# Closing TensorE's loop in the middle of an output slot, and alternating short and full pieces in the second score fill

## The chip, the core and the metric

The kernel runs on one core of a Trainium2 chip. The metric is the time of one execution on the device in microseconds (us). Repeats of one kernel scatter by 0.1 to 1%.

## The reference

```python
B, H, Sq, Sk, D = 16, 32, 192, 1024, 128          # bf16
def reference(q, k, v):
    scores = jnp.einsum("bhqd,bhkd->bhqk", q, k) * D ** -0.5
    return jnp.einsum("bhqk,bhkd->bhqd", softmax(scores), v)
```

There are 512 heads. The kernel treats four at a time, a *quad*, so there are 128 quads.

## The kernel before

For each quad, TensorE makes three *score fills*. A fill computes 512 columns of scores (keys on the partitions, queries along the columns) for each of the four heads into four PSUM banks. A column block of 192 queries of one key tile does not divide 512, so the fills are cut into pieces; `CUTS` lists them as (key tile, first query, end query). Between the fills stand *value slots*: half a quad's outputs need 1.5 slots, so there are three slots a quad too. ScalarE takes the exponential of each fill (one instruction for the bank of the first head, one for the other three), VectorE normalizes each slot's output.

The lines that matter, shortened (`step(f)` is written out as its two calls, "..." marks what is left out):

```python
CUTS = (
    ((0, 0, 192), (1, 0, 192), (2, 0, 128)),
    ((2, 128, 192), (3, 0, 192), (4, 0, 192), (5, 0, 64)),     # the second fill
    ((5, 64, 192), (6, 0, 192), (7, 0, 192)),
)
...
def take(s, c):
    pe.wait_ge(s, c).then_inc(s, -c)
def qk(f):                                    # a score fill
    x, b = divmod(f, 3)
    if b == 0:
        take(s_qt, 1)
    take(s_kt, 1)
    take(s_e1, 1)                             # the first head's bank has been read
    for t, n0, n1 in CUTS[b]:
        for w in range(4):                    # one pass: four matmuls, 32 rows each, one per head
            for a in range(4):
                ins = pe.matmul(S[:, c0: c0 + n1 - n0], kt[...], qt[...], start=w == 0, ...)
    ins.then_inc(s_qk, 1)
def pv(s):                                    # a value slot: 32 matmuls in pairs of 64 columns
    x, i = divmod(s, 3)
    if i == 0:
        take(s_e3, 3)                         # the exps of this quad
        take(s_vp, 2)                         # its values
    ...
        take(s_on, 1)                         # the last slot has been normalized
    ...
    ins.then_inc(s_pv, 1)
with nc.Fori(0, NF // (3 * R), engines=[PE], head_slot={PE: 100}):
    for f in range(3 * R):                    # two quads in one turn of the loop
        qk(f)
        pv(f - LAG)                           # LAG = 4: the slot that follows fill 1 begins a quad
```

Each `take` is one instruction of TensorE's *sequencer*, the part of the engine that works through waits, takes and branches and hands the matmuls to TensorE's queue. And the slot that follows the second fill is the one with `i == 0`: three takes (the exps, the spread values, the normalized slot) stand between that fill and that slot, where the other fills have one.

## Time and profile before

| | before |
|---|---|
| median, range | 841.78 us, 841.64 to 842.84 (3 runs) |
| span of the profiled run | 840.2 us |
| TensorE busy, ScalarE busy | 98%, 89% |
| quad to quad, quads 4 to 90 | 6.329 us |

First the page of the profile: a busy line (us, share of the span, instructions), the DMA rate in 40 slices of the span, and groups of instructions (busy time, mean ns of one, then the engine's idle time before them and what ended most of it). L613 is the fills' matmul, L632 the slots', L777 and L780 are the exps.

```profile
PE 821.0 (98%) x32910; PEld 735.3 (88%) x32910; DVE 599.6 (71%) x1288; ACT 748.4 (89%) x770; POOL 549.9 (65%) x646
GB/s 329 399 401 404 404 404 406 403 405 401 389 400 401 392 401 386 397 396 399 386 392 392 391 400 400 382 400 401 382 400 396 392 398 392 394 389 397 393 159 43
L780 ACT ACTIVATE f_pt<-f_s 128x1536 bf16<-128x1536 f32 x384 | 554.9, 1445 | 0.0
L632 PE MATMUL f_o<-f_vp,f_pt 128*64 128x129 bf16 x12320 | 433.5, 222 | 3.0 <-issue 2.9
L613 PE MATMUL f_s<-f_qt,f_kt 32*128 32x192 bf16 (+2 forms) x20480 | 423.6, 226 | 6.6 <-PEq L597 3.8
L777 ACT ACTIVATE f_pt<-f_s 128x512 bf16<-128x512 f32 x384 | 229.2, 597 | 79.3 <-PE f_s L613 71.3
```

TensorE has next to no idle time and ScalarE waits for it, so TensorE sets the pace. But "busy" here counts from the first matmul's start to a modelled end, so short holes between matmuls hide in it. The timeline of TensorE around one turn of the loop shows them (columns: start us, duration us, engine, line, what, how many):

```profile
407.85 1.09 PE L613 MATMUL f_s<-f_qt,f_kt 32*128 32x128 bf16 x48
408.87 1.13 PE L632 MATMUL f_o<-f_vp,f_pt 128*64 128x129 bf16 x32
409.99 1.10 PE L613 MATMUL f_s<-f_qt,f_kt 32*128 32x192 bf16 x48
411.02 1.11 PE L632 MATMUL f_o<-f_vp,f_pt 128*64 128x129 bf16 x32
412.06 1.11 PE L613 MATMUL f_s<-f_qt,f_kt 32*128 32x64 bf16 x64
413.17 0.34 PE L632 MATMUL f_o<-f_vp,f_pt 128*64 128x129 bf16 x5
```

The durations overlap; the starts are what counts. From slot to next fill is 411.02 to 412.06 = 1.04 us in a plain place, but 408.87 to 409.99 = 1.12 us where the loop closes. And the second fill (x64) takes 412.06 to 413.17 = 1.11 us, where the first takes 1.03 and the third 1.02, for the same 2048 query columns per head.

In the rest of this text a *gap* is the time from the start of the last matmul of a fill or slot to the start of the first one of the next, by the start times in the trace, averaged over quads 30 to 125. Within a fill, passes start 85 ns apart for 192 queries, 57 for 128 and 29 for 64.

### The profile page before, as it was taken

Reading aid. Unit: us, or ns where it says so; the run is one execution under the profiler, and the core shown is the slowest. Engines: PE = TensorE matmul, PEld = TensorE weight load, DVE = VectorE, ACT = ScalarE, POOL = GpSimd, SP = SyncE. Lnnn points to the kernel's source line nnn. Section 1 sums busy time; section 2 is a strip of 40 time slices with the busy share of each in tenths; the row PEclk is TensorE's granted clock in tenths of the full one; section 3 lists DMA queues with packets and bytes.
Section 4 is the critical chain, followed back from the end, with each engine's and each line's share of the span. In section 5 each row is a group of like instructions: output and inputs, shape, how many; then the busy total and the mean of one; then the engine's idle time right before and its main releaser. Section 6 shows DMA issues by size and latency. Waiting matters only on the chain. (4 is left out here: it accounts for less than half of the span.)

```text
span 840.2 us, 71522 instructions
## 1 busy us (share of the span) xinstructions
PE 821.0 (98%) x32910; PEld 735.3 (88%) x32910; DVE 599.6 (71%) x1288; ACT 748.4 (89%) x770; POOL 549.9 (65%) x646
## 2 busy tenths in 40 slices
PE   6999999999999999999999999999999999999995
PEld 4789898988888989988988888988998998888885
DVE  5577777777777777777777777777777777777763
ACT  5699999999999999999999999999999999999994
POOL 6566666666666766766766666666666666676671
PEclk9899999999999999999999999999999999999999
DMA  8999999999999999999999999999999999999941
GB/s 329 399 401 404 404 404 406 403 405 401 389 400 401 392 401 386 397 396 399 386 392 392 391 400 400 382 400 401 382 400 396 392 398 392 394 389 397 393 159 43
DMA packets 139213, 319.21 MB, mean 380 GB/s; under 512 B 7200, under 2 KB 57376, under 8 KB 122912
## 3 DMA queue, kind: packets, MB, share of 16 engines
q1 hardware_dynamic: 139168, 318.80, 99.3%
q14 instruction: 39, 0.32, 0.1%
q8 instruction: 6, 0.10, 0.1%
HBM read 293.60 MB, written 25.17 MB: 379 GB/s over the span
## 5 line engine op out<-in xcount | busy, mean ns | idle before, releaser
L780 ACT ACTIVATE f_pt<-f_s 128x1536 bf16<-128x1536 f32 x384 | 554.9, 1445 | 0.0
L571 POOL COPY f_kt<-f_kx 128x768 uint32<-128x768 uint32 (+1 forms) x384 | 293.7, 784 | 269.9 <-DVE f_kx L696 140.7
L632 PE MATMUL f_o<-f_vp,f_pt 128*64 128x129 bf16 x12320 | 433.5, 222 | 3.0 <-issue 2.9
L613 PE MATMUL f_s<-f_qt,f_kt 32*128 32x192 bf16 (+2 forms) x20480 | 423.6, 226 | 6.6 <-PEq L597 3.8
L632 PEld LDWEIGHTS f_o<-f_vp,f_pt 128*64 128x64 bf16 x12320 | 373.3, 110 | 46.2 <-issue 24.0
L613 PEld LDWEIGHTS f_s<-f_qt,f_kt 32*128 32x128 bf16 x20480 | 357.7, 92 | 46.5 <-issue 10.1
L696 DVE STREAM_TRANSPOSE f_kx<-f_kn 128x768 uint32<-128x768 uint32 (+1 forms) x384 | 334.0, 870 | 10.5 <-DMA f_kn<-in_k_dram 10.5
L777 ACT ACTIVATE f_pt<-f_s 128x512 bf16<-128x512 f32 x384 | 229.2, 597 | 79.3 <-PE f_s L613 71.3
L580 POOL COPY f_vp<-f_vs 128x1024 uint32<-128x1024 uint32 x256 | 259.5, 1043 | 5.1 <-PE f_o L632 5.0
L717 DVE RECIPROCAL f_rinv<-f_o 128x2 f32<-128x2 f32 x381 | 65.1, 171 | 206.6 <-PE f_o L632 206.6
L721 DVE TENSOR_TENSOR f_ob<-f_o,f_rinv 128x256 bf16<-128x256 f32 x381 | 161.7, 424 | 13.3 <-DVE f_rinv L717 0.3
L705 DVE STREAM_TRANSPOSE f_qt<-f_qn 128x384 uint32<-128x384 uint32 x128 | 72.8, 569 | 0.0
L661 PE MATMUL f_o<-f_ones 128*128 128x512 bf16 x12 | 4.1, 512 | 1.1 <-POOL f_ones L562 1.1
L661 PEld LDWEIGHTS f_o<-f_ones 128*128 128x128 bf16 x12 | 1.4, 127 | 3.2 <-issue 1.7
L677 DVE MEMSET f_pt<- 128x3072 uint32 x1 | 2.6, 2618 | 1.5 <-PEq L806 1.5
L563 POOL MEMSET f_vp<- 128x4160 uint32 x1 | 3.6, 3569 | 0.0
L632 PE MATMUL f_s<-f_vp,f_pt 128*64 128x129 bf16 x96 | 3.2, 220 | 0.3 <-PEq L597 0.3
L632 PEld LDWEIGHTS f_s<-f_vp,f_pt 128*64 128x64 bf16 x96 | 2.9, 110 | 0.4 <-issue 0.4
L769 ACT ACTIVATE f_pt<-f_ones 128x3072 f32<-128x3072 bf16 x1 | 2.8, 2763 | 0.0
L769 ACT ACT_TABLE_LOAD x1 | 1.3, 1283 | 0.8 <-PEq L806 0.8
L717 DVE RECIPROCAL f_rinv<-f_s 128x2 f32<-128x2 f32 x3 | 0.5, 171 | 1.4 <-PE f_s L632 1.4
L671 PE MATMUL f_o<-f_bad,f_ones 128*1 128x1 bf16 x1 | 0.2, 164 | 1.3 <-DVEq L761 1.3
(13 smaller groups left out, 5.3 us busy)
## 6 DMA issues: line engine op xcount, KB each, us to landing
f_vs<-in_v_dram SPq DMA_DIRECT2D x128, 1024.0 KB, 9.0
f_kn<-in_k_dram SPq DMA_DIRECT2D x127, 1024.0 KB, 11.1
f_qn<-in_q_dram SPq DMA_DIRECT2D x128, 192.0 KB, 10.3
out_dram<-f_ob SPq DMA_DIRECT2D x63, 384.0 KB, 11.4
f_kn<-in_k_dram SPq DMA_DIRECT2D x1, 640.0 KB, 6.7
f_kn<-in_k_dram SPq DMA_DIRECT2D x1, 384.0 KB, 3.9
out_dram<-f_ob SPq DMA_DIRECT2D x2, 192.0 KB, 2.3
```

The source lines that it names most:

```text
L571: gp.tensor_copy(kt[:, x % NKT].bitcast(U32).rearrange("p U (j s u) c -> p U j s (u c)", s=2, u=2)[:, lo:hi], kx[:, x % 2].rearrange("p (U ...
L580: gp.tensor_copy(vp[:, x % NVP, 2 * T * i: 2 * T * i + 2 * T, 0:D].bitcast(U32), vs[:, x % NVS, 2 * i: 2 * i + 2, :].rearrange("p a (t d) ...
L613: ins = pe.matmul(S[:, c0: c0 + n1 - n0], kt[r, x % NKT, 2 * t + h, :, c], qt[r, x % R, h, n0:n1, c], start=w == 0, stop=w == 3, tile_posi ...
L632: return pe.matmul(O[m0: m0 + m, u, 0:129], pt[:, x % R, 2 * y + z, t * SQ + n0: t * SQ + n0 + m], vp[:, x % NVP, (2 * y + z) * T + t, 0:129],
L661: pe.matmul(o_ps[:].rearrange("p a b -> p (a b)"), ones[:], ones[:].unsqueeze(1).to_broadcast([128, 4, 128]), start=True, stop=True)
L696: dve.transpose(kx[:, x % 2].rearrange("p (U s j u) -> p s u U j", s=2, j=32, u=2)[:, :, :, lo:hi], kn[:, x % NKN].rearrange("p (s u U i) ...
L705: dve.transpose(qt[:, x % R].bitcast(U32).rearrange("p b (y j u) c -> p u y b (j c)", y=3, u=2), qn[:, x % NKN].rearrange("p (u y b i) -> ...
L717: dve.reciprocal(ri, O[:, :, 128]).then_inc(s_rc, 1)
L721: dve.tensor_tensor(ob[:, so, 6 * a + 2 * w: 6 * a + 2 * w + 2, :], O[:, :, 0:128], ri.unsqueeze(2).to_broadcast([128, 2, D]), ALU.mult,). ...
L769: act.activation(pt[:, 1].rearrange("p a c -> p (a c)").bitcast(F32), ones[:, 0:1].to_broadcast([128, 2 * T * SQ]), ACT_FN.Copy).then_inc( ...
L777: act.activation(pt[:, x % R, 0, c], s1_ps[:], ACT_FN.Exp, scale=scale).then_inc(s_e1, 1)
L780: act.activation(pt[:, x % R, 1:4, c], s3_ps[f % 2][:], ACT_FN.Exp, scale=scale).then_inc(s_e3, 1)
```

## The change

The intent is to hide two costs of TensorE's sequencer. (The diff is shortened; the first and third line of `CUTS` get the same nesting and keep their order.) The loop's register step and branch now stand between the two halves of a value slot, so that queued matmuls cover them. And the second fill no longer ends with four short passes in a row: its passes alternate, full (192 queries), short (64), full, short, so that the last passes last longer. No matmul is added or removed in the steady part; an extra half slot runs once at the start, and one is made up for behind the loop. The thresholds on `s_pv` rise by one (`BLANK`) for the blank slot.

```diff
-    ((2, 128, 192), (3, 0, 192), (4, 0, 192), (5, 0, 64)),
+    (((3, 0, 192), (2, 128, 192)), ((4, 0, 192), (5, 0, 64))),
...
+    BLANK = LAG + 1
...
-                    for t, n0, n1 in CUTS[b]:
-                        c0 = t * SQ + n0 - 512 * b
+                    for group in CUTS[b]:
                         for w in range(4):
...
+                            for g, (t, n0, n1) in enumerate(group):
+                                c0 = t * SQ + n0 - 512 * b
+                                for a in range(4):
...
-                                    start=w == 0, stop=w == 3, tile_position=(32 * a, 0))
+                                        start=w == 0 and g == 0, stop=w == 3, skip_group_check=True,
+                                        tile_position=(32 * a, 0))
...
-                def pv(s):
+                def pv(s, blocks=(0, 1)):
...
-                    ins.then_inc(s_pv, 1)
+                    if 1 in blocks:
+                        ins.then_inc(s_pv, 1)
...
+                    pv(-1 - LAG, (1,))
                     for f in range(3 * R):
-                        step(f)
-                for f in range(NF, NF + LAG):
-                    step(f)
+                        qk(f)
+                        pv(f - LAG, (0,) if f == 3 * R - 1 else (0, 1))
+                pv(NF - 1 - LAG, (1,))
+                for s in range(NF - LAG, NF):
+                    pv(s)
```

## The prediction

> **What bounds the kernel.** TensorE. The page's busy line gives PE 98%, ACT 89%, DVE 71%, POOL 65%. In the steady part (windows 40 to 790 us) PE is busy 99.9% at granted clock 1.00. Successive quads of heads (three fills each) start 6.33 us apart in the trace. ScalarE is a close second: its two exps take 597 + 1445 ns a fill, 6.13 us a quad, and before the first it waits 0.15 to 0.21 us for TensorE's scores (timeline at 400 to 420). DMA moves 393 to 404 GB/s and looks full, but K lands about 10 us before its transpose in mid-run, and that lead grew while DMA ran at 404: about 6.15 us a quad is its floor. So TensorE can gain about 0.18 us a quad before another wall.
>
> **Where TensorE loses time.** Start times of single matmuls show steady passes: 85 ns for 192 queries, 57 for 128, 29 for 64, 59 for a pair of value matmuls. Each switch between score tiles (32 rows) and value tiles (64 columns) costs about 90 ns beyond the last pass. The Trainium skill, "TensorEngine Tiling (Array Packing)", section "Key Properties", says that changing the tiling mode drains TensorE; these gaps agree. Two gaps are longer than the drain, because the sequencer is late:
> 1. *Loop edge.* Value slot to score fill takes 225 ns (mean) from last matmul start to first where the loop closes, 153 elsewhere. The sequencer gets there only 340 ns into the value slot, because the queue holds it back; then come a 102 ns register step, a 207 ns branch and three semaphore takes of about 150 ns. Loss 72 ns x 64 = 4.6 us.
> 2. *After the second fill.* Three takes follow it. The sequencer leaves the fill 260 ns before its last matmul starts, because the queue then holds the last six passes (two of 85, four of 29). The gap is 161 ns, where 29 + 90 = 118 would do. Loss 43 ns x 128 = 5.5 us.
>
> **What the change does.** It adds and removes no matmuls in the loop (half a dummy slot before the first fill, about 0.5 us, hidden under the first load). At the edge only half a slot (32 instructions) is queued before the branch, so the sequencer should reach it without queueing, run the branch under the queued matmuls, and catch up: the first gap goes to about 153 ns, 4.6 us saved. Alternating makes the last six passes three of 85 and three of 29, 56 ns longer, so the takes are ready before the drain ends: second gap 118 to 130 ns, 4 to 5.5 us. The fill itself (919 to 924 ns, first to last matmul) stays or loses about 10 ns. Everything else waits on TensorE and follows; ACT's idle time shrinks, DMA needs about 399 GB/s.
>
> **Sum.** All of it is on the critical path; about 122 of 128 quads are in the steady part. 8 to 11 us at best; I take 9: **832.8 us**, range 828.5 to 837.5. Chances: faster by over 2% 0.02, within 2% 0.96, slower 0.02.
>
> **What shows each step.** Quad period 6.25 us instead of 6.33; loop-edge gap 153; gap after second fill under 130; ACT's idle before its first exp down from 79 us to about 70; DMA 398 to 400 GB/s in mid-run; busy times of ACT, DVE and POOL unchanged.
>
> **What would make it wrong.** Half a slot is too little cover and TensorE starves in mid-slot after the branch (a hole of tens of ns between the halves); alternating 192- and 64-query passes breaks the 29 ns pace, because a weight load no longer hides under a short pass; instruction fetch stalls elsewhere in the rotated loop; or an exp becomes late and its wait replaces the gap.

## The result, and the profile after

The changed kernel takes 837.22 us (median of 4 runs, 836.53 to 839.74), against 841.71 us before in the same rounds. The ratio is 0.995, with a 95% interval of 0.9927 to 0.9973. A ratio is the mean time of one kernel's fast runs over that of the other's of the same rounds, so it is not quite the ratio of the medians. The gain is 4.5 us, where 9 were forecast.

The page of the changed kernel, the lines that answer to those above (L616 fills, L638 slots, L782 and L785 exps):

```profile
PE 818.2 (98%) x32926; PEld 726.0 (87%) x32926; DVE 599.3 (72%) x1288; ACT 748.6 (90%) x770; POOL 550.0 (66%) x646
L785 ACT ACTIVATE f_pt<-f_s 128x1536 bf16<-128x1536 f32 x384 | 554.6, 1444 | 1.8 <-PE f_o L638 1.8
L638 PE MATMUL f_o<-f_vp,f_pt 128*64 128x129 bf16 x12336 | 434.3, 222 | 1.8 <-issue 1.8
L616 PE MATMUL f_s<-f_qt,f_kt 32*128 32x192 bf16 (+2 forms) x20480 | 421.6, 226 | 5.9 <-issue 3.4
L782 ACT ACTIVATE f_pt<-f_s 128x512 bf16<-128x512 f32 x384 | 229.3, 597 | 72.6 <-PE f_s L616 37.8
```

Its TensorE timeline around one turn of the loop:

```profile
405.56 1.09 PE L616 MATMUL f_s<-f_qt,f_kt 32*128 32x128 bf16 x48
406.58 1.13 PE L638 MATMUL f_o<-f_vp,f_pt 128*64 128x129 bf16 x32
407.64 1.10 PE L616 MATMUL f_s<-f_qt,f_kt 32*128 32x192 bf16 x48
408.67 1.11 PE L638 MATMUL f_o<-f_vp,f_pt 128*64 128x129 bf16 x32
409.72 1.09 PE L616 MATMUL f_s<-f_qt,f_kt 32*128 32x192 bf16 x64
410.79 0.42 PE L638 MATMUL f_o<-f_vp,f_pt 128*64 128x129 bf16 x8
```

The slot in which the loop closes now lasts 406.58 to 407.64 = 1.06 us instead of 1.12: that half of the change did what it should. The second fill lasts 409.72 to 410.79 = 1.07 us. By the forecast of fill and gap it was to come down to 1.03 to 1.05.

The two stretches from the start of quad 4 to that of quad 124 contain nearly the whole difference. In the windows view (start:end, length, then busy us and instructions of each engine, granted clock, DMA share, GB/s) the kernel before and then the changed one:

```profile
43.02:802.29 759.27, 758.66 (x30723) 682.00 (x30721) 556.87 (x1200) 697.88 (x721) 511.69 (x601) 1.00 1.03 396
```

```profile
42.74:797.62 754.88, 754.86 (x30723) 672.70 (x30721) 556.65 (x1200) 697.87 (x721) 511.76 (x602) 1.00 1.04 399
```

The same work (30723 matmuls, ScalarE 697.9 us) fits in 4.4 us less. The clock was full in both.

### The profile page after: what moved, and what is told of

The parts are those of the page before. It is cut to its first block, busy times and chain, and to the rows that moved or that the text cites. A ratio compares the mean times of both kernels' runs of the same rounds, so it can differ in the third digit from the quotient of the medians.

```text
span 835.6 us, 71554 instructions
## 1 busy us (share of the span) xinstructions
PE 818.2 (98%) x32926; PEld 726.0 (87%) x32926; DVE 599.3 (72%) x1288; ACT 748.6 (90%) x770; POOL 550.0 (66%) x646
## 2 busy tenths in 40 slices
DMA packets 139213, 319.21 MB, mean 382 GB/s; under 512 B 7200, under 2 KB 57376, under 8 KB 122912
## 5 line engine op out<-in xcount | busy, mean ns | idle before, releaser
L785 ACT ACTIVATE f_pt<-f_s 128x1536 bf16<-128x1536 f32 x384 | 554.6, 1444 | 1.8 <-PE f_o L638 1.8
L638 PE MATMUL f_o<-f_vp,f_pt 128*64 128x129 bf16 x12336 | 434.3, 222 | 1.8 <-issue 1.8
L616 PE MATMUL f_s<-f_qt,f_kt 32*128 32x192 bf16 (+2 forms) x20480 | 421.6, 226 | 5.9 <-issue 3.4
L638 PEld LDWEIGHTS f_o<-f_vp,f_pt 128*64 128x64 bf16 x12336 | 373.9, 110 | 53.7 <-issue 23.5
L616 PEld LDWEIGHTS f_s<-f_qt,f_kt 32*128 32x128 bf16 x20480 | 347.6, 92 | 43.0 <-issue 6.5
L782 ACT ACTIVATE f_pt<-f_s 128x512 bf16<-128x512 f32 x384 | 229.3, 597 | 72.6 <-PE f_s L616 37.8
L638 PE MATMUL f_s<-f_vp,f_pt 128*64 128x129 bf16 x96 | 3.1, 220 | 0.3 <-PEq L599 0.3
L638 PEld LDWEIGHTS f_s<-f_vp,f_pt 128*64 128x64 bf16 x96 | 2.9, 110 | 0.4 <-issue 0.4
```

The lines of the kernel that those rows point to most:

```text
L616: ins = pe.matmul(S[:, c0: c0 + n1 - n0], kt[r, x % NKT, 2 * t + h, :, c], qt[r, x % R, h, n0:n1, c], start=w == 0 and g == 0, stop=w == 3 ...
L638: return pe.matmul(O[m0: m0 + m, u, 0:129], pt[:, x % R, 2 * y + z, t * SQ + n0: t * SQ + n0 + m], vp[:, x % NVP, (2 * y + z) * T + t, 0:129],
L782: act.activation(pt[:, x % R, 0, c], s1_ps[:], ACT_FN.Exp, scale=scale).then_inc(s_e1, 1)
L785: act.activation(pt[:, x % R, 1:4, c], s3_ps[f % 2][:], ACT_FN.Exp, scale=scale).then_inc(s_e3, 1)
```

## The experiments

All times below are medians. This table has what the traces and the times gave; the gaps are means over quads 30 to 125, ns. Each ratio is to the kernel before in the same rounds.

| kernel | gap at the loop edge | second fill, first to last start | gap after it | quad, 4 to 90, us | time, us | ratio to before |
|---|---|---|---|---|---|---|
| before | 225 | 921 | 161 | 6.329 | 841.71 | 1 |
| the changed kernel | 153 | 904 | 169 | 6.291 | 837.22 | 0.995 |
| its repeat, after_again | 153 | 904 | 169 | 6.291 | 837.40 | 0.9948 |
| edge_only | 153 | 923 | 167 | 6.304 | 838.60 | 0.9965 |
| alt_only | 209 | 905 | 169 | 6.318 | 841.94 | 1.0003 |
| head_132 | 211 | 921 | 155 | 6.319 | 841.34 | 0.9999 |
| short_last | 153 | 918 | 386 | 6.518 | 866.67 | 1.0299 |
| short_first | 153 | 865 | 171 | 6.248 | 834.78 | 0.9917 |
| extra_wait | 153 | 904 | 169 | 6.291 | 838.05 | 0.9954 |
| extra_take | 153 | 905 | 321 | 6.434 | 855.79 | 1.0166 |
| takes_first | 153 | 905 | 115 | 6.234 | 834.10 | 0.9903 |
| takes_first_again | 153 | 905 | 115 | 6.234 | 834.36 | 0.9913 |
| takes_edge | 153 | 924 | 117 | 6.252 | 834.35 | 0.9919 |
| takes_half_v (wrong result) | 153 | 905 | 115 | 6.234 | 831.94 | 0.9884 |

One more source of scatter must be known to read the last two columns together: the start, while the first loads arrive. In the traces the fifth quad (quad 4) began between 42.7 us (the changed kernel) and 45.3 us (extra_take) after the span's start; two traces of the very same changed kernel had 42.7 and 44.3. A kernel may gain 1.3 us in its quads and show nothing in its time.

### Each half alone: edge_only and alt_only

edge_only is the changed kernel with the second fill in its old order:

```diff
-    (((3, 0, 192), (2, 128, 192)), ((4, 0, 192), (5, 0, 64))),
+    (((2, 128, 192),), ((3, 0, 192),), ((4, 0, 192),), ((5, 0, 64),)),
```

> Only the loop's closing point is moved; the second fill keeps the old order of its pieces (64, 192, 192, 64). If the two halves of the change add up, the gap at the loop edge is 153 ns as in the changed kernel, the gap after the second fill stays at the 161 ns of the kernel before (151 to 183), the quad period is about 6.29 us, and the time 838 us, 0.995 to 0.996 of before. If the alternation brought a real share of the 4.5 us, this kernel is 1 to 4 us slower than the changed one.

alt_only is the kernel before with the changed `CUTS` and the changed loop in `qk`, and nothing else.

> Only the second fill alternates; the loop closes at the end of a value slot as before. Expected: loop-edge gap 211 to 254 ns as before, second fill 904 ns from first to last matmul start and a gap of 169 ns after it as in the changed kernel, period about 6.32 us, time 840 to 841.5 us. Over 2 us gained would mean that the alternation is worth something by itself.

They ran in the same rounds as a repeat of the changed kernel:

> The changed kernel once more, on the same chip and in the same rounds as the three others, as their yardstick: 837 us, 0.995 of before.

The repeat took 837.40 us, 0.9948 (0.9934 to 0.9963). edge_only took 838.60 us, 0.9965 (0.9953 to 0.9977), with the loop-edge gap at 153 ns. The trace's records of the sequencer show the cover (means over the 48 loop edges of quads 30 to 125). In the kernel before, the register step begins 340 ns into the slot, the branch ends 650 ns in, and the last take begins 1023 ns in, 117 ns after the slot's last matmul. In the changed kernel these are 22, 332 and 789 ns, and the last take begins 119 ns before the slot's last matmul. alt_only took 841.94 us, 1.0003 (0.999 to 1.0016). In the quads the parts add up nearly: 6.329 to 6.304 (25 ns) for the edge, 6.329 to 6.318 (11 ns) for the alternation, 38 ns for both. So the loop edge brought most of the gain, and the alternation about 11 ns a quad, 1.3 us in the quads of its trace. Its time does not show even that; its profiled run reached quad 4 at 44.4 us, against 43.0 before, and lost as much there.

Those 11 ns are not the ones that were forecast, and the shorter fill did not bring them either. The fill became 17 ns shorter and the gap after it 8 ns *longer*: as the experiments below show, in both kernels the slot starts when the takes are done, wherever the fill ends before that. From the fill's first matmul to the slot's first one it takes 1082 ns before and 1073 ns in the changed kernel. The first take comes at the same time in both (662 and 660 ns). What differs is the two spacings between the three takes: together 314 ns before, where some takes are spaced 186 ns instead of 156, and 307 ns in the changed kernel, where none are. In alt_only the gaps at the loop edge became regular too (209 ns instead of 225 in the mean). The next experiment gets nearly the same without alternating.

### Is it the place in the fetch blocks? head_132

Moving the loop's closing point also moves every instruction of the loop against its head. `head_slot` sets the place at which the loop's first instruction stands in the block of instructions in which it is loaded. The kernel before, with the head 32 places later:

```diff
-                             head_slot={mybir.EngineType.PE: 100}):
+                             head_slot={mybir.EngineType.PE: 132}):
```

> The kernel before with its loop's first instruction loaded 32 places later in the fetch block, so that nearly all of the loop stands in the blocks as it does in the changed kernel. If the gain at the loop edge is the cover of queued matmuls, nothing changes: edge gaps 211 to 254 ns, 841 to 842 us. If it came from where the instructions fall in the blocks, the edge gap falls toward 153 ns and the time toward 837 us. The irregular quads (6.42 us instead of 6.35) may change in number: worth under 1.5 us.

The edge gap is 211 ns, far from 153, and the time 841.34 us, 0.9999 (0.9983 to 1.0016). So the gain at the edge comes from the cover; this one other place does not bring it. The place has a small effect of its own. At slot 100, 15 of 48 edge gaps of the kernel before are about 254 ns and the rest about 210; at 132 only one is that long. And at 132 no take after the second fill is spaced 186 ns instead of 156, so that fill and gap last 1076 ns together instead of 1082. In the quads that is worth 10 ns, which is what alt_only gained (6.319 and 6.318 us). Either change makes the sequencer's steps regular; beyond that, alternation is not shown to bring more than the 3 ns between 1076 and 1073. Why the steps are irregular is open: edge_only, whose instructions stand in the same places as those of the changed kernel, has such takes too (its two spacings are 321 ns together).

### What the gap after the second fill waits for: takes_first and extra_take

The gap is 169 ns. Theory 1: the sequencer comes late, because three takes stand there. Rival: this is the *drain*, the time that TensorE needs between the last pass of score tiles and the first of value tiles, and it is that long when a full pass stands just before the last short one. takes_first moves two of the takes ahead of the fill, where the sequencer has to wait for the exp anyhow:

```diff
                     take(s_kt, 1)
+                    if b == 1:
+                        take(s_e3, 3)
+                        take(s_vp, 2)
                     take(s_e1, 1)
...
-                    if i == 0:
+                    if i == 0 and s >= NF - LAG:
                         take(s_e3, 3)
                         take(s_vp, 2)
```

> The changed kernel, with the takes of the third exps and of the spread values moved from behind the second fill to ahead of it, so that one take is left between the fill and its value slot. Theory 1 (the gap of 169 ns is the sequencer, late by two takes): the gap falls to about 118 ns, the period to 6.24 us, the time to about 831 us, 0.987 of before. Rival (169 ns is what TensorE needs to drain when a 192-query pass stands just before the last short pass): the gap stays at 169 ns and the time at 837 us.

The gap fell to 115 ns in every quad, and the quads to 6.234 us. The timeline of TensorE in it, the second fill and what follows:

```profile
408.05 1.09 PE L619 MATMUL f_s<-f_qt,f_kt 32*128 32x192 bf16 x64
409.07 1.13 PE L641 MATMUL f_o<-f_vp,f_pt 128*64 128x129 bf16 x32
```

From the fill to the slot it is now 1.02 us. Theory 1 holds and the rival falls. (The one take that is left comes 777 ns into the fill, later than the first of the three did. It is the take of the normalized slot, whose normalization ends 739 ns in. The value slot starts only 243 ns after it, so it costs nothing.) The time is 834.10 us, 0.9903 (0.9883 to 0.9923), 3 us more than expected; that is the subject of takes_half_v.

The opposite dose is one more wait in that place. The first attempt changed nothing:

```diff
                         take(s_vp, 2)
+                        pe.wait_ge(s_one, 1)
```

> The changed kernel with one more wait, long satisfied, between the second fill and its value slot. If the sequencer is what the gap waits for, each thing added to it shows in full: the gap grows from 169 ns by the wait's own cost, 50 to 150 ns, and the time by 128 times that, 6 to 19 us. If the gap is TensorE's drain, with the sequencer only just in time by chance, it grows as well but by less than the wait's spacing in the trace.

The gap stayed at 169 ns, the time at 838.05 us. The trace shows why: no instruction was added. The wait was joined to the take that follows (`take(s_on)`), which then waits for two semaphores at no visible cost. So the test did not test; mended, with a count so that it has to stand alone:

```diff
+                        pe.wait_ge(s_one, 1).then_inc(s_dum, 1)
```

> The dose test again, mended: the single added wait of the run before made no instruction of its own. Here one more long satisfied take, which also counts up a semaphore that nobody reads, stands between the second fill and its value slot of the changed kernel. If the gap waits for the sequencer, it grows by one take's spacing, from 169 to about 320 ns, and the time by about 128 x 0.151 = 19 us, to about 857 us. If the gap is the drain, with the takes hidden inside it, it grows by less than 100 ns and the time by less than 13 us.

```profile
407.71 1.09 PE L617 MATMUL f_s<-f_qt,f_kt 32*128 32x192 bf16 x64
408.94 0.77 PE L640 MATMUL f_o<-f_vp,f_pt 128*64 128x129 bf16 x20
```

From the fill to the slot it is now 1.23 us: the gap grew from 169 to 321 ns, one take's spacing in full. The quad grew by 143 ns (6.291 to 6.434 us; some 10 ns came back in other fills and slots), and the time to 855.79 us. So nearly all of each take in this place is paid for, in each of the 128 quads.

### When the sequencer can leave a fill: short_last and short_first

That leaves the question why alternating did not bring the takes forward. In the trace's records of the sequencer, the first take after the second fill comes 662 ns after the fill's first matmul before, and 660 ns after it in the changed kernel. The forecast wanted it some 56 ns earlier, relative to the last matmul. One theory: the queue lets the sequencer go at a certain pass. Rival: the sequencer needs a fixed time for the fill's 128 instructions. The two tests put all short passes last, and all first:

```diff
-    (((3, 0, 192), (2, 128, 192)), ((4, 0, 192), (5, 0, 64))),
+    (((3, 0, 192),), ((4, 0, 192),), ((2, 128, 192),), ((5, 0, 64),)),     # short_last
+    (((2, 128, 192),), ((5, 0, 64),), ((3, 0, 192),), ((4, 0, 192),)),     # short_first
```

> The changed kernel with the order of the second fill's pieces 192, 192, 64, 64: all eight short passes last. Theory (the sequencer can leave the fill only some 105 ns after its tenth pass has started, because until then the queue is full): the tenth pass is then a short one, starting about 720 ns into the fill, the first take comes at about 825 ns, the value slot starts about 414 ns after that, so the gap after the fill is about 335 ns, 21 us more in all: about 858 us. Rival (the sequencer needs a fixed time for the fill's 128 instructions, 957 ns after the take that lets it in, whatever TensorE does): first take at 660 ns as now, gap 168 ns, 837 us.

> The changed kernel with the order 64, 64, 192, 192: all eight short passes first. Theory of the full queue: the tenth pass starts about 330 ns into the fill, the first take comes at about 435 ns, the takes are over long before the fill is, and the gap is the drain alone after a 192-query pass, 171 ns as after the third fill, with the last matmul starting 850 ns after the first instead of 904; the period falls by about 50 ns to 6.24 us, the time to 831 us. Rival of the fixed time: first take at 660 ns and value slot at 1073 ns as now, 837 us. If the short passes at the start find the queue empty, they run slower than 29 ns each, and part of the gain is lost: then 832 to 836 us.

In short_last it is 1.30 us from the second fill to the slot, and the profile itself now calls the rest a wait for the sequencer ("PEq"):

```profile
411.77 1.11 PE L616 MATMUL f_s<-f_qt,f_kt 32*128 32x192 bf16 x64
413.07 0.74 PE L638 MATMUL f_o<-f_vp,f_pt 128*64 128x129 bf16 x19 [0.19 <-PEq L599]
```

The time is 866.67 us, 1.0299 (1.0284 to 1.0314). The first take comes 886 ns into the fill. In short_first it comes 465 ns in, long before the fill's end, and the gap of 171 ns is the drain alone; the time is 834.78 us, 0.9917 (0.9892 to 0.9943). The rival of the fixed time (660 ns in all orders) falls. (831 us were expected, or 832 to 836 if the short passes began slowly. They did: the first ones start 40 and 32 ns apart instead of 29, and the fill lasts 865 ns instead of 850. Its quads run at 6.248 us up to quad 90 and at 6.304 us from 90 to 124, where it waits for K as takes_first does below.)

My number was off, though: 335 ns of gap were expected in short_last, and 386 came. The four orders together say at which pass the sequencer is let go. Of the passes' starts, that of the ninth of the 16 lies at the most even distance from the take. It starts at (ns after the first matmul), and the first take comes at (differences taken before rounding):

| order of the second fill | 9th pass starts | first take | difference |
|---|---|---|---|
| before | 474 | 662 | 187 |
| alternating | 468 | 660 | 191 |
| short passes last | 695 | 886 | 192 |
| short passes first | 251 | 465 | 214 |

Measured from the tenth pass the differences would scatter from 103 to 164 ns, from the eighth from 221 to 276. So it is the ninth pass, not the tenth: when the take comes, the matmuls of the last eight passes have not ended, or not for more than 10 ns, by the trace's modelled ends. That is 32 matmuls and their 32 weight loads. The Trainium skill, "TensorE: Matmul & The Clock Gate", gives TensorE a queue of 64 entries in the table at its head; these runs agree with 64 if an entry is held until its matmul has ended, which the page doesn't say and no run shows directly.

With that the gap can be worked out. After the first take come two more spacings (156 + 151 ns), then 107 ns to the first value matmul, by the records of before and after. The slot can start 187 + 307 + 107 = 601 ns after the ninth pass at the earliest. Before: 474 + 601 - 921 = 154 ns (161 measured, the mean with some takes spaced 186 ns). Changed: 468 + 605 - 904 = 169 ns (169). Short passes last: 695 + 606 - 918 = 383 ns (386). The 605 and 606 are 601 with those orders' own differences, 191 and 192 ns, in place of 187.

In both the old order and the alternating one, the last eight passes are four full and four short. Alternating shuffles them within the queue's reach and so cannot give the sequencer more time.

### Where takes_first lost its last 3 us: takes_half_v and takes_edge

takes_first ran its quads at 6.234 us up to quad 90 and at 6.351 us from 90 to 124. The lines of the windows view for 100 to 300 and 600 to 780 us, and the wait of VectorE's transposes for K (total us, times, longest):

```profile
100.00:300.00 200.00, 199.98 (x8210) 178.72 (x8204) 148.69 (x320) 186.61 (x194) 136.97 (x162) 1.00 1.04 404
600.00:780.00 180.00, 177.48 (x7273) 158.42 (x7264) 132.61 (x285) 164.88 (x171) 120.75 (x143) 1.00 1.03 393
```

```profile
DVE f_kx L704 <- DMA f_kn<-in_k_dram: 25.3, 32, 3.4
```

TensorE's busy time falls below its window in the second stretch, and DMA moves 393 GB/s. Worked out from the 319.21 MB of the page, quads of 6.234 us need 400. K landed 6 to 8 us before its use from quad 6 to quad 54, the lead then shrank by about 0.2 us a quad, and from quad 96 on it was 0.02 us: the transposes waited for each load. The test takes a fifth of the traffic away, with a wrong result on purpose (relative error 0.91):

```diff
+                    g = 4 if x < NVS else 2
                     e.dma_start(
-                        vs[:, x % NVS, :, :],
-                        vf[4 * x:4 * x + 4].rearrange("a (m t) d -> m a (t d)", t=T),
+                        vs[:, x % NVS, 0:g, :],
+                        vf[4 * x:4 * x + g].rearrange("a (m t) d -> m a (t d)", t=T),
```

> Wrong result on purpose: the version with two takes moved ahead of the second fill, loading only half of V from the sixth quad on, so that DMA has a fifth less to move. That version ran at 6.23 us a quad until K's lead was used up near quad 90, then at 6.35. If DMA is the wall that it met, the quads stay at 6.23 to 6.24 us to the end, K's lead stays above 5 us, and the time is 829 to 831 us with little scatter. If something else stretched those quads (the stores' buffers, ScalarE, the vector engine), they are as long as before and the time is about 834 us.

```profile
600.00:780.00 180.00, 180.00 (x7408) 160.94 (x7402) 134.51 (x290) 167.94 (x174) 122.92 (x145) 1.00 0.93 317
```

```profile
DVE f_kx L705 <- DMA f_kn<-in_k_dram: 10.3, 5, 3.3
```

The quads stay at 6.23 us to the end, K's lead at 12 to 15 us, and the later waits for K are gone; the 10.3 us that are left, in five waits, are the start's, as in the kernel before, which has this line:

```profile
DVE f_kx L696 <- DMA f_kn<-in_k_dram: 10.5, 5, 3.5
```

DMA is the wall. The time, 831.94 us, 0.9884 (0.9866 to 0.9901), is 1 us above the expected range; its profiled run came late out of the start (quad 4 at 44.9 us).

The last pair asks whether the alternation is worth anything when the sequencer is in time. takes_edge has the takes moved, the loop closed in mid-slot, and the old order of the fill:

> The two takes moved ahead of the second fill and the loop closed in mid-slot, but the second fill in its old order 64, 192, 192, 64: is the alternation worth anything once the sequencer is no longer late? Expected: gap after the second fill about 118 ns, from first to last matmul of the fill 921 ns against 904, so quads of about 6.25 us until DMA's lead is used up, and a time within 2 us of the alternating one (832 to 836 us).

It ran beside a repeat of takes_first:

> The alternating version with the two takes ahead of the fill once more, as the yardstick of these rounds, on the chip that they run on: 831 to 836.5 us; quads of 6.23 us as long as K's lead lasts.

takes_edge took 834.35 us, 0.9919 (0.9901 to 0.9936), the repeat 834.36 us, 0.9913 (0.9886 to 0.994). The quads still differ by 18 ns as long as the lead lasts (6.252 and 6.234 us), but with DMA at its limit the times are the same. takes_first beats the changed kernel of the same rounds, 0.9903 against 0.9948 with intervals that do not meet.

## Why the prediction was right and wrong

The time fell inside the range (837.22 us; 828.5 to 837.5), but only by 0.3 us and at its slow end, and the gain of 4.5 us was half of the 9 forecast. Point by point:

- **TensorE bounds the kernel, and its gaps are the place to look: right.** ScalarE's idle time before its first exp fell from 79.3 to 72.6 us (about 70 forecast), DMA moved 399 GB/s (398 to 400), the busy times of ScalarE, VectorE and GpSimd did not change.
- **"the first gap goes to about 153 ns, 4.6 us saved": right.** It went from 225 to 153 ns, and the loop's step and branch now run under queued matmuls. Alone it brought 25 ns a quad in the trace and 2.6 us by the medians, less than 36 ns and 4.6 us, in part since in that trace the second fill and the gap after it grew a little (921 to 923 and 161 to 167 ns).
- **"The sequencer leaves the fill 260 ns before its last matmul starts, because the queue then holds the last six passes": wrong, and this is the step that failed.** The 260 ns were read correctly and explained wrongly. The take comes about 190 ns after the ninth pass starts, when by the four orders the last *eight* passes are still outstanding. "Alternating makes the last six passes three of 85 and three of 29, 56 ns longer" is true, but of the last eight there are four and four in either order. I took the pass that happened to start at the moment of the take for the one that released it, and one order of passes cannot tell the two apart. So "second gap 118 to 130 ns, 4 to 5.5 us" came out as 169 ns, and the second fill with its gap brought 9 ns a quad, about 1.1 us in 120 quads.
- **The gap could be 118 ns: right.** takes_first reached 115. The cause named, takes behind the fill, was right; the remedy did not act on it.
- **The fill "stays or loses about 10 ns": roughly right**, it lost 17. But as long as the takes are late this shortens nothing: 8 ns went back into the gap, and the other 9 are the more regular takes (7 ns) and a first take 2 ns earlier. Only where the takes are in time does a shorter fill count (takes_edge and takes_first, 924 and 905 ns, quads of 6.252 and 6.234 us).
- **"about 6.15 us a quad is its floor" for DMA: wrong.** 404 GB/s was kept only in the early part. In takes_first, landings of K from quad 4 to 126 came 6.32 us apart on average. It did not matter for the changed kernel, whose lead was 8 to 10 us from quad 30 on, but the wall stood much nearer than the 0.18 us that I gave.

Adding up in the quads: 36 ns from the edge (72 every second quad), 9 from the earlier start of the slot after the second fill (1082 to 1073 ns), less some 7 ns in the other fills and slots, make 38 ns; times 120 quads that is 4.5 us.

Still open: why some takes and edges of the kernel before take 30 to 45 ns longer, and why either another order or another place of the loop's head removes that; why DMA's rate falls after the first 300 us, and whether an entry of the queue is freed by the end of a matmul.

## What to carry to other kernels

When an engine's sequencer is late, look for the event that lets it go and count instructions from there; an order of work changes nothing unless it changes what stands behind that event, and two or three different orders are needed to find which event it is. Put semaphore instructions where the sequencer waits anyhow, and loop branches where enough work is queued. Before valuing a gain beyond the next wall, measure that wall over the whole run, not where it looks best.

## What the Trainium skill lacked or had wrong

- "TensorE: Matmul & The Clock Gate", the specification table: a queue of 64 with a partial reorder window, but not what holds an entry. In four orders of a fill of 128 instructions the sequencer reached the next instruction 187 to 214 ns after the ninth of 16 passes started, with the last 32 matmuls and their loads not yet ended, or for at most 9 ns, by the modelled ends.
- "TensorEngine Tiling (Array Packing)", section "Key Properties": says that a change of tiling mode drains TensorE, but gives no cost. Here the gap from 32-row to 64-column tiles was 115, 143 and 171 ns after passes of 29, 57 and 85 ns: about 86 ns beyond the last pass.
- "Advanced Engine Details and Errata", section "Control Flow Timing": compare-and-branch about 108 ns. In the kernel before, the loop's branch back is recorded with 207 to 208 ns, and begins 102 ns after the start of the register step.
- No page has the cost of a semaphore take on TensorE: successive takes stood 151 to 156 ns apart, and one more between two tile modes lengthened the gap by 152 ns, while a wait that was joined to a following take cost nothing (gap 169 ns with and without).
